# Wider DMA rows for q, k and the first values of a fused attention and feed-forward kernel

## The chip, the cores and the metric

One Trainium2 chip, one core. The metric is the device time of one execution in microseconds (us). Each kernel is executed several times, and each time is compared with runs of the kernel before on the same chip. Most kernels were also profiled once; span, timeline and waits come from that one execution.

## The reference

```python
def _attn_ref(q, k, v):                       # q, k, v: (8, 8, 576, 64) float32
    B, H, S, D = q.shape; chunk = 64; nc = S // chunk
    ...                                       # q_c, k_c, v_c: reshaped to (B, H, nc, chunk, D)
    scores = scale * np.matmul(q_c, k_c.transpose(0, 1, 2, 4, 3))
    ...                                       # softmax over the 64 keys of the chunk
    out = np.matmul(attn, v_c)

def _moe_ref(x, w_in, w_out):                 # x: (4608, 512), w_in: (512, 2048), w_out: (2048, 512)
    h = np.maximum(x @ w_in, 0.0)
    return (h * h @ w_out).astype(np.float32)
```

Every chunk of 64 tokens attends to itself alone. The outputs of the 8 heads are laid side by side as x, and x goes through the feed-forward network.

## The kernel before

The kernel takes the tokens in groups of 256. For each group it loads q, k and v, transposes q and k on TensorE, computes scores, their exponential (ScalarE), the value products (TensorE), the division (VectorE), and the transpose of x; then it runs the feed-forward matmuls for blocks of two groups. Groups 0 and 1 are done ahead of all feed-forward work ("the prologue"); the others are slipped between feed-forward matmuls. `keep_busy(n)` issues n matmuls of the identity, whose results nobody reads ("fillers").

For groups 0 to 3, q and k are each a tile of all 128 partitions, two tokens to a partition, so that each head gives a row of 512 B in DRAM:

```python
def qk_pieces(g):
    q_sb = in_pool.tile([128, 2, H, D], FP32, name="q_sb")
    k_sb = in_pool.tile([128, 2, H, D], FP32, name="k_sb")
    ...
            for dst, src in ((q_sb, q), (k_sb, k)):
                yield lambda ...: nc.sync.dma_start(
                    out=dst...[p:p + m // 2, :]...,
                    in_=src[b, :, s:s + m, :].rearrange("h (s i) d -> s h (i d)", i=2))
```

Values come in rows of 256 B, one token each, and the value products take 64 keys, that is 64 rows of the array, at a time:

```python
        for t in tiles:
            ...
            for hp in range(n_hp):
                for a in range(2):
                    for p in range(2):
                        c = p ^ a
                        vb = vob[t + p] if a else veb[:, t]
                        nc.tensor.matmul(
                            out=ps[64 * p:64 * p + 64, a, hp * (D + 1):(hp + 1) * (D + 1)],
                            lhsT=e[64 * c:64 * c + 64, a, hp, t, :],
                            rhs=vb[64 * c:64 * c + 64, hp, 1::2], start=True, stop=True)
            ...
            nc.vector.reciprocal(out=rec, in_=o[:, :, :, D])      # the sum, from a column of ones
            nc.vector.tensor_tensor(... op=ALU.mult)
```

The prologue, in TensorE's program order (TE: transposes of q and k; SC: scores; AV: value products of a tile of 128 tokens):

```python
    go(pieces([0, 1]))
    load_w_in(0, n_cast=2)
    TE(0); keep_busy(8); SC(0); keep_busy(6)
    TE(1); keep_busy(8); SC(1); keep_busy(10)
    AV(0, [0]); keep_busy(4); AV(0, [1]); keep_busy(8)
    transpose_x_early(0, 0); keep_busy(10); transpose_x_early(0, 1)
    AV(1, [0]); keep_busy(8); AV(1, [1])
    transpose_x_early(1, 0); keep_busy(14); transpose_x_early(1, 1); keep_busy(10)
```

The softmax here doesn't subtract the row's maximum and nothing guards it: scores larger than these inputs give would overflow.

Of the kernel before, what the change touches and what calls it, by code (L numbers as in the profile page):

```python
# [10 lines left out]
FP32 = mybir.dt.float32  # L11
# [6 lines left out]
def kernel(  # L18
# [19 lines left out]
    GT = 256  # L38
    n_grp = n_tokens // GT

    blocks = [[0, 1], [3, 2]] + [[g, g + 1] for g in range(4, n_grp, 2)]
    FIRST_DMA_T = 4
    FIRST_DMA_X = 6
    BT = GT * max(len(b) for b in blocks)
# [22 lines left out]
    NO = 2 * NV + 1  # L67
    v_even = [w_pool.tile([128, 2, n_hp, D + 1], FP32, name=f"ve_sb{i}") for i in range(NV)]
    v_odd = [w_pool.tile([128, n_hp, D + 1], FP32, name=f"vo_sb{i}") for i in range(NO)]
    for vt in v_even:  # L70
        nc.gpsimd.memset(vt[:, :, :, D:D + 1], 1.0)
    for vt in v_odd:
# [12 lines left out]
    def runs(g):  # L85

        for t in range(GT // 128):
            p = 0
            for b, s, m in segments(g * GT + t * 128, 128):
                yield t, p, m, b, s  # L90
                p += m

    def qk_pieces(g):
        q_sb = in_pool.tile([128, 2, H, D], FP32, name="q_sb")
        k_sb = in_pool.tile([128, 2, H, D], FP32, name="k_sb")
        qk[g] = (q_sb, k_sb)
        if g < FIRST_DMA_T:

            p = 0
            for b, s, m in segments(g * GT, GT):  # L100
                for dst, src in ((q_sb, q), (k_sb, k)):
                    yield lambda dst=dst, src=src, b=b, s=s, p=p, m=m: nc.sync.dma_start(  # L102
                        out=dst.rearrange("p t h d -> p (t h d)")[p:p + m // 2, :].rearrange(
                            "p (h e) -> p h e", h=H),
                        in_=src[b, :, s:s + m, :].rearrange("h (s i) d -> s h (i d)", i=2))
                p += m // 2
            return
        for t, p, m, b, s in runs(g):
            for dst, src in ((q_sb, q), (k_sb, k)):
                yield lambda dst=dst, src=src, b=b, s=s, t=t, p=p, m=m: nc.sync.dma_start(  # L110
                    out=dst[p:p + m, t, :, :],
                    in_=src[b, :, s:s + m, :].rearrange("h s d -> s h d"))

    def v_pieces(g):

        for t, p, m, b, s in runs(g):
            yield lambda t=t, p=p, m=m, b=b, s=s: nc.sync.dma_start(  # L117
                out=v_even[g % NV][p:p + m, t, :, 0:D],
                in_=v[b, 0::2, s:s + m, :].rearrange("h s d -> s h d"))
        for n in {0: [0, 1, 2], 2: [5], 3: [6, 7, 8]}.get(g, [2 * g + 1, 2 * g + 2]):  # L120
            lo, hi = max(0, 128 * n - 64), min(n_tokens, 128 * n + 64)
            p = lo - (128 * n - 64)
            for b, s, m in segments(lo, hi - lo):
                yield lambda n=n, p=p, m=m, b=b, s=s: nc.sync.dma_start(  # L124
                    out=v_odd[n % NO][p:p + m, :, 0:D],
                    in_=v[b, 1::2, s:s + m, :].rearrange("h s d -> s h d"))
                p += m
# [25 lines left out]
            place[g] = (j, i * GT)  # L153
    state = {}

    def transpose_paired(g, which, psb):

        src = qk[g][which].bitcast(BF16).rearrange(
            "p t h d -> p (t h d)").rearrange("p (h i d) -> p h i d", h=H, i=2)
        dst = psb.rearrange("c (h i q) -> c h i q", h=n_hp, i=2)  # L160
        for hp in range(n_hp):
            for i in range(2):
                for a in range(2):
                    nc.tensor.transpose(
                        out=dst[64 * a:64 * a + 64, hp, i, :],
                        in_=src[:, 2 * hp + a, i, 1::2],
                        identity=ident)

    def copy_paired(copy, qkT, psb):
        src = psb.rearrange("c (h i t p) -> c t h p i", h=n_hp, i=2, t=2)  # L170
        dst = qkT.rearrange("c t h (p i) -> c t h p i", i=2)
        for t in range(2):
            copy(out=dst[:, t], in_=src[:, t])

    def transpose_qk(g, q_pool, k_pool):
        qkT = att_pool.tile([128, 2, 2, n_hp, 128], BF16, name="qkT", bufs=4)
        state["qkT", g] = qkT
        for which, pool in enumerate((q_pool, k_pool)):
            copy = nc.scalar.copy if which else nc.vector.tensor_copy
            if pool is ps_ffn:  # L180
                bank = pool.tile([128, 512], FP32, name="ps_ffn")
            else:
                bank = pool.tile([128, 1024], FP32, name="ps_att")
            bank = bank.bitcast(BF16)[:, 0:1024]
            transpose_paired(g, which, bank)
            copy_paired(copy, qkT[:, which], bank)

    def transpose_x_early(g, t):
        j, c = place[g]
# [33 lines left out]
    def scores(g):  # L223
        qkT = state.pop(("qkT", g))
        ps = ps_att.tile([128, 1024], FP32, name="ps_att")
        for hp in range(n_hp):
            for t in range(2):
                for a in range(2):
                    for p in range(2):
                        c = p ^ a  # L230
                        cols = slice(p * 64, p * 64 + 64)
                        o0 = a * 512 + hp * 128 + t * 64
                        nc.tensor.matmul(  # L233
                            out=ps[64 * c:64 * c + 64, o0:o0 + 64],
                            lhsT=qkT[64 * a:64 * a + 64, 1, t, hp, cols],
                            rhs=qkT[64 * a:64 * a + 64, 0, t, hp, cols],
                            start=True, stop=True)
        e = att_pool.tile([128, 2, n_hp, 2, 64], BF16, name="e")
        state["e", g] = e
        nc.scalar.activation(  # L240
            out=e.rearrange("p a h t q -> p (a h t q)"), in_=ps, func=AF.Exp, scale=scale)

    def values(g, tiles=(0, 1)):
# [5 lines left out]
        x = state["x", g]  # L249
        for t in tiles:  # L250
            ps = ps_att.tile([128, 2, 512], FP32, name="ps_att")
            for hp in range(n_hp):
                for a in range(2):
                    for p in range(2):
# [5 lines that stand above are left out]
                            rhs=vb[64 * c:64 * c + 64, hp, 1::2],  # L260
                            start=True, stop=True)
# [30 lines left out]
    SC, AV, XT = scores, values, transpose_x  # L292

    def TA(g):
        transpose_qk(g, ps_att, ps_att)

    def TE(g):
        transpose_qk(g, ps_ffn, ps_ffn)

    def TM(g):  # L300
        transpose_qk(g, ps_att, ps_ffn)

    def XE(g):
        for t in range(2):
# [80 lines left out]

    go(pieces([0, 1]))
    load_w_in(0, n_cast=2)
    TE(0)
    keep_busy(8)
    SC(0)  # L390
# [112 lines left out]
```

## Time and profile before

| | before |
|---|---|
| time, median of 3 runs | 299.43 us (298.48 to 302.96) |
| the profiled execution | 296.57 us, span 294.8 us |
| first feed-forward matmul | 20.40 us |
| from there to the end | 274.4 us |

### The profile page before, as it was taken

How to read it: one execution, taken by the hardware profiler on the slowest of the kernel's cores; microseconds unless marked ns; L12 is line 12 of the kernel's file. 1: busy time of each engine (PE TensorE's matmuls, PEld its weight loads, DVE VectorE, ACT ScalarE, POOL GpSimd, SP SyncE). 2: the span in 40 equal slices, each digit the busy share in tenths (PEclk: the TensorE clock that was granted, in tenths of full speed). 3: DMA queues.
4: the chain of work that ended last, by engine and by line, in shares of the span. 5: the costliest groups of instructions: out<-in, count | busy, mean ns of one | idle time of the engine just before them, and what ended most of it. 6: DMA issues, size and time to landing. Idle time of an engine off the chain costs nothing.

```text
span 294.8 us, 6460 instructions
## 1 busy us (share of the span) xinstructions
PE 282.4 (96%) x2630; PEld 142.2 (48%) x2630; DVE 112.5 (38%) x246; ACT 130.9 (44%) x226; POOL 67.8 (23%) x103
## 2 busy tenths in 40 slices
PE   2999999899999999999999999999999999999994
PEld 1774445786454444444444444444444444444441
DVE  1157713594334520461047106720661046104300
ACT  1526514684327612771276127612761276126411
POOL 2027834050060052034104213311221100110010
PEclk9999999999999999999999999999999999999999
DMA  7999999999999999999999899799997401210011
GB/s 200 236 316 361 345 326 209 279 225 201 231 220 222 228 230 226 237 196 194 250 225 207 198 275 234 126 174 277 246 161 161 130 36 38 71 73 36 0 71 71
DMA packets 156140, 57.03 MB, mean 193 GB/s; under 512 B 139280, under 2 KB 151824, under 8 KB 156112
## 3 DMA queue, kind: packets, MB, share of 16 engines
q1 hardware_dynamic: 153168, 47.33, 77.5%
q0 software_dynamic: 2800, 9.18, 9.1%
q8 instruction: 20, 0.33, 0.5%
q10 hardware_dynamic: 144, 0.13, 0.1%
q14 instruction: 8, 0.07, 0.1%
HBM read 36.70 MB, written 9.44 MB: 157 GB/s over the span
## 4 chain that ended last, share of the span: by engine, by line
PE 74%; DMA 10%; SPq 8%; DVE 3%; issue 2%; ACT 1%; POOL 1%; ACTq 0%
PE ps_ffn L332 36%; PE ps_ffn L316 34%; DMA w_st<-in_moe_w_in_dram 5%; DMA k_sb<-in_k_dram 2%; SPq L124 2%; SPq L102 2%; DMA w_st<-in_moe_w_out_dram 2%; DVE gT L323 2%; PE ps_att L257 2%; SPq L117 2%; PE ps_att L233 1%; DMA qkT<-qkb 1%; ACT rl L322 1%; DVE x L265 1%; POOL w_in_bf L139 1%
## 5 line engine op out<-in xcount | busy, mean ns | idle before, releaser
L316 PE MATMUL ps_ffn<-xT,w_in_bf 128*128 128x512 bf16 (+1 forms) x640 | 128.9, 358 | 0.2 <-ACT rl L322 0.2
L323 DVE TENSOR_TENSOR gT<-rl 128x512 bf16<-128x512 bf16 (+1 forms) x160 | 75.3, 488 | 128.0 <-ACT rl L322 126.2
L332 PE MATMUL ps_ffn<-w_out_bf,gT 128*128 128x512 bf16 x512 | 112.9, 379 | 0.0
L322 ACT ACTIVATE rl<-ps_ffn 128x512 bf16<-128x512 f32 (+1 forms) x160 | 86.6, 557 | 37.7 <-PE ps_ffn L316 33.8
L316 PEld LDWEIGHTS <-w_in_bf 128*128 128x128 bf16 x640 | 61.0, 98 | 60.0 <-issue 0.5
L332 PEld LDWEIGHTS <-gT 128*128 128x128 bf16 x512 | 49.3, 98 | 58.0
L349 ACT COPY o_sb<-ps_ffn 128x512 f32<-128x512 f32 x31 | 18.2, 586 | 91.5 <-PE ps_ffn L332 91.5
L350 POOL DMA_DIRECT2D out_dram<-o_sb x31 | 16.7, 540 | 130.6 <-ACT o_sb L349 123.9
L212 POOL CAST qkb<-q_sb 128x1024 bf16<-128x1024 f32 x14 | 14.9, 1066 | 58.0 <-DMA q_sb<-in_q_dram 47.3
L265 DVE TENSOR_TENSOR x<-ps_att,rec 128x512 bf16<-128x512 f32 x36 | 24.9, 691 | 1.2
L240 ACT ACTIVATE e<-ps_att 128x1024 bf16<-128x1024 f32 x18 | 17.8, 1024 | 4.8 <-PE ps_att L233 4.8
L212 POOL CAST qkb<-k_sb 128x1024 bf16<-128x1024 f32 x14 | 15.2, 1082 | 2.4 <-DMA k_sb<-in_k_dram 2.1
L361 PE MATMUL ps_ffn<-w_out_bf,gT 128*128 128x512 bf16 x64 | 14.7, 379 | 0.0
L139 POOL CAST w_in_bf<-w_st 128x1024 bf16<-128x1024 f32 (+1 forms) x9 | 9.0, 1002 | 19.5 <-DMA w_st<-in_moe_w_in_dram 19.5
L264 DVE RECIPROCAL rec<-ps_att 128x8 f32<-128x8 f32 x36 | 7.1, 198 | 16.0 <-PE ps_att L257 16.0
L147 POOL CAST w_out_bf<-w_st 128x1024 bf16<-128x1024 f32 x8 | 9.0, 1122 | 6.0 <-DMA w_st<-in_moe_w_out_dram 5.8
L257 PEld LDWEIGHTS <-e 64*64 64x64 bf16 x576 | 6.4, 107 | 7.2 <-ACT rl L322 1.7
L361 PEld LDWEIGHTS <-gT 128*128 128x128 bf16 x64 | 6.0, 98 | 7.2 <-issue 0.3
L257 PE MATMUL ps_att<-ve_sb,e 64*64 64x65 bf16 x288 | 8.7, 196 | 0.1
L233 PEld LDWEIGHTS <-qkT 64*64 64x64 bf16 x576 | 6.0, 110 | 5.7 <-issue 4.2
L257 PE MATMUL ps_att<-vo_sb,e 64*64 64x65 bf16 x288 | 8.7, 196 | 0.0
L233 PE MATMUL ps_att<-qkT 64*64 64x64 bf16 x576 | 7.7, 197 | 1.0 <-DMA qkT<-qkb 0.6
(34 smaller groups left out, 55.0 us busy)
## 6 DMA issues: line engine op xcount, KB each, us to landing
out_dram<-o_sb POOLq DMA_DIRECT2D x35, 256.0 KB, 3.6
q_sb<-in_q_dram SPq DMA_DIRECT2D x25, 256.0 KB, 4.9
k_sb<-in_k_dram SPq DMA_DIRECT2D x25, 256.0 KB, 4.9
ve_sb<-in_v_dram SPq DMA_DIRECT2D x32, 128.0 KB, 4.0
vo_sb<-in_v_dram SPq DMA_DIRECT2D x32, 128.0 KB, 3.9
w_st<-in_moe_w_in_dram SPq DMA_DIRECT2D x8, 512.0 KB, 7.3
w_st<-in_moe_w_out_dram SPq DMA_DIRECT2D x8, 512.0 KB, 6.1
q_sb<-in_q_dram SPq DMA_DIRECT2D x3, 512.0 KB, 6.7
```

The costliest lines, as they stand in the source:

```text
L212: nc.gpsimd.tensor_copy(out=qkb[:, which], in_=qk[g][which].rearrange("p t h d -> p (t h d)"))
L233: nc.tensor.matmul(out=ps[64 * c:64 * c + 64, o0:o0 + 64], lhsT=qkT[64 * a:64 * a + 64, 1, t, hp, cols], rhs=qkT[64 * a:64 * a + 64, 0, t, ...
L240: nc.scalar.activation(out=e.rearrange("p a h t q -> p (a h t q)"), in_=ps, func=AF.Exp, scale=scale)
L257: nc.tensor.matmul(out=ps[64 * p:64 * p + 64, a, hp * (D + 1):(hp + 1) * (D + 1)], lhsT=e[64 * c:64 * c + 64, a, hp, t, :], rhs=vb[64 * c: ...
L265: nc.vector.tensor_tensor(out=x[:, t].rearrange("p h a d -> p a h d"), in0=o[:, :, :, 0:D], in1=rec.to_broadcast([128, 2, n_hp, D]), op=AL ...
L316: nc.tensor.matmul(out=h[:, 0:n], lhsT=w_in_bf[:, dt, ft * 128:(ft + 1) * 128], rhs=xT[:, c // 128:(c + n) // 128, dt, :], start=(dt == 0) ...
L322: nc.scalar.activation(out=rl[:, 0:n], in_=h[:, 0:n], func=AF.Relu)
L323: nc.vector.tensor_tensor(out=gT[:, ft, c:c + n], in0=rl[:, 0:n], in1=rl[:, 0:n], op=ALU.mult)
L332: nc.tensor.matmul(out=o_ps, lhsT=gT[:, ft, tt * 128:(tt + 1) * 128], rhs=w_out_bf[:, ft, :], start=(ft == 0), stop=(ft == n_ft - 1))
L349: nc.scalar.copy(out=o_sb, in_=o_ps)
L350: nc.gpsimd.dma_start(out=out[t0:t0 + 128, :], in_=o_sb)
L361: nc.tensor.matmul(out=o_ps[tt], lhsT=gT[:, ft, tt * 128:(tt + 1) * 128], rhs=w_out_bf[:, ft, :], start=(ft == 0), stop=(ft == n_ft - 1))
```

## The change

The intent is fewer and longer DMA rows, so that the first loads land sooner. For groups 0 to 3, q and k share a tile, q in partitions 0 to 63 and k in 64 to 127, with four tokens to a partition and rows of 1 KB. For groups 0 and 1, the values come in rows of 512 B of two tokens; the keys of a chunk then lie in 32 partitions as even and odd ones, so that scores and value products are done with 32-key tiles and accumulated, on top of a product of zeros that opens the accumulation, and the two halves of the sum are added by VectorE. Forty fillers are put ahead of the first transposes. The core of the diff:

```diff
     def qk_pieces(g):
-        q_sb = in_pool.tile([128, 2, H, D], FP32, name="q_sb")
-        k_sb = in_pool.tile([128, 2, H, D], FP32, name="k_sb")
+        qk_sb = in_pool.tile([128, 2, 2, H, D], FP32, name="qk_sb")
...
-                for dst, src in ((q_sb, q), (k_sb, k)):
...
-                        in_=src[b, :, s:s + m, :].rearrange("h (s i) d -> s h (i d)", i=2))
-                p += m // 2
+                for p0, src in ((p, q), (64 + p, k)):
+                    yield lambda dst=qk[g], src=src, b=b, s=s, p=p0, m=m: nc.sync.dma_start(
+                        out=dst[p:p + m // 4],
+                        in_=src[b, :, s:s + m, :].rearrange("h (s i) d -> s h (i d)", i=4))
+                p += m // 4
...
     def v_pieces(g):
+        if g < N_PAIRED:                      # N_PAIRED = 2
...
+                yield lambda b=b, s=s, p=p, m=m: nc.sync.dma_start(
+                    out=v_pair[g][p:p + m // 2, :, 1:2 * D + 1],
+                    in_=v[b, :, s:s + m, :].rearrange("h (s i) d -> s h (i d)", i=2))
...
     def scores(g):                            # 64 products of 32 keys for 32 of 64 keys
...
     def values(g, tiles=(0, 1)):
+            if g < N_PAIRED:
...
+                        nc.tensor.matmul(     # 2 x 2 of these
+                            out=ps[64 * p:64 * p + 64, a, 0:n_hp * E],
+                            lhsT=zeros[rows, 0:64], rhs=zeros[rows, 0:n_hp * E],
+                            start=True, stop=False)
...
+                                nc.tensor.matmul(   # 4 x 2 x 2 x 2 of these
+                                    out=ps[64 * p:64 * p + 64, a, hp * E + i:hp * E + i + D + 1],
+                                    lhsT=e[rows, a, hp, i, :],      # rows: 32 partitions
+                                    rhs=vp[rows, 2 * hp + a, ...],
+                                    start=False, stop=(i == 1 and hp == n_hp - 1))
...
+                nc.vector.tensor_copy(out=rec, in_=o[:, :, :, 0])
+                nc.vector.tensor_tensor(out=rec, in0=rec, in1=o[:, :, :, D + 1], op=ALU.add)
                 nc.vector.reciprocal(out=rec, in_=rec)
...
     load_w_in(0, n_cast=2)
+    keep_busy(40)
     TE(0)
```

## The prediction

> **What bounds the kernel now.** I read the page's shares first, then the chain of work that ended last, then TensorE's waits in the first 80 us, then the timeline up to 21 us. TensorE is busy 282.4 of 294.8 us. From 20.40 us on it runs the feed-forward matmuls almost without a hole, so two things remain to a change at the start: when that dense stretch begins, and the few waits after it. The waits of TensorE in 0 to 80 us, longest first (total us, times, longest):

> ```profile
> PE ps_ffn L164 <- DMA q_sb<-in_q_dram: 5.0, 1, 5.0
> PE ps_ffn L164 <- DMA k_sb<-in_k_dram: 1.8, 2, 1.1
> PE ps_att L233 <- DMA qkT<-qkb: 0.6, 1, 0.6
> ```

> 5.0 us is the first load; of the 1.8 us, 0.7 is the first k and 1.1 is the k of group 2, at 52.65 us. The prologue, in the timeline (start, us, engine, line):

> ```profile
> 5.02 1.06 PE L164 MATMUL ps_ffn<-ident,q_sb 128*64 128x128 bf16 x16 [5.02 <-DMA q_sb<-in_q_dram]
> 6.83 1.06 PE L164 MATMUL ps_ffn<-ident,k_sb 128*64 128x128 bf16 x16 [0.74 <-DMA k_sb<-in_k_dram]
> 7.82 1.03 PE L206 MATMUL ps_ffn<-ident 128*128 128x128 bf16 x8
> ...
> 10.33 1.06 PE L164 MATMUL ps_ffn<-ident,q_sb 128*64 128x128 bf16 x16
> ...
> 12.15 0.62 PE L206 MATMUL ps_ffn<-ident 128*128 128x128 bf16 x8
> ...
> 14.81 0.21 DVE L264 RECIPROCAL rec<-ps_att 128x8 f32<-128x8 f32 x1 [2.08 <-PE ps_att L257]
> ...
> 15.05 0.69 DVE L265 TENSOR_TENSOR x<-ps_att,rec 128x512 bf16<-128x512 f32 x1
> ...
> 20.40 13.97 PE L316 MATMUL ps_ffn<-xT,w_in_bf 128*128 128x512 bf16 x64
> ```

> See three things. Eight fillers take 1.03 us early and 0.62 us at 12.15: TensorE is slow until about 12 us. The transposes of group 1 start at 10.33 without waiting on a load, so up to there TensorE's own queue set the pace. And from the first value product (14.40 us) to the feed-forward there are 6.0 us, a chain product, VectorE, transpose, copy. Then the load rates, in stretches of 1 or 2 us (the last column is GB/s; q and k, then values, then w_in):

> ```profile
> 5.00:6.00 1.00, 0.98 (x16) 0.82 (x16) 0.00 (x0) 0.00 (x0) 0.00 (x0) 1.00 1.20 289
> 12.00:13.00 1.00, 0.87 (x18) 0.56 (x14) 0.73 (x2) 0.73 (x2) 0.00 (x0) 1.00 1.31 210
> 22.00:24.00 2.00, 2.00 (x11) 0.89 (x10) 1.34 (x3) 1.25 (x3) 1.61 (x2) 1.00 1.10 362
> 46.00:48.00 2.00, 2.00 (x41) 1.01 (x40) 0.00 (x0) 1.51 (x2) 0.00 (x0) 1.00 1.13 193
> ```

> 512 B rows run at 289 GB/s, 256 B rows at 210, the 1 KB rows of w_in at 362. The last is the stretch in which values and the q, k of group 2 queue.

> [...]per engine and packet they are 19.5, 28 and 45 ns for 256, 512 and 1024 B, a line with some 10 ns at zero. [...]The q and k of group 2 come as pieces of 32 and 96 partitions in the same 512 B rows. From issue plus time to landing they land at 48.36 (q, 32), 48.95 (k, 32), 50.74 (q, 96), 52.54 us (k, 96): 128 KB in 0.59 us is 222 GB/s, 384 KB in 1.80 us is 218, against 289 for whole tiles.[...]

> **The change, part by part.**

> 1. *q, k in 1 KB rows.* Half the packets, and by rows alone 1 MB would take 2.9 us at 362 GB/s instead of 3.6 us. But q goes to partitions 0 to 63 and k to 64 to 127, one transfer after the other. By the pieces above I take 220 to 235 GB/s: 4.5 us per group. Landings before, issue plus time to landing: q0 4.94, k0 6.74, q1 8.55, k1 10.47 us. After: the flow starts 1.8 us before 4.94, at 3.1; k0 lands at 7.6 and k1 at 12.1 us. Every first transpose now holds q and k rows, so it waits for k0, where before it began with q0 at 5.02.

> 2. *Fillers.* The identity is ready at 1.66 us. 40 fillers at 0.107 us end at 6.0. They replace idle time and cost nothing, but with k0 at 7.6 they stop short of it.

> 3. *Transposes and copies.* 32 transposes per group as before; one copy of 1024 columns instead of two of 512 on each engine. I count 1.2 us on VectorE (two took 1.29) and 1.05 on ScalarE (1.07): nothing.

> 4. *Scores of groups 0, 1.* 64 matmuls instead of 32. 64 took 0.64 us together in later blocks: +0.3 us each.

> 5. *Values in 512 B rows.* 1.0 MB instead of 1.06 MB, at 289 instead of 210 GB/s: 3.6 instead of 5.1 us. With k1 at 12.1, v0 lands at 13.9, v1 at 15.7, the first w_in at 17.2 instead of 18.1. So the later loads come 0.9 us sooner. This pays only if something waits for them.

> 6. *Value products.* Before, 16 matmuls per tile in four array tiles, stepping 0.04 us per four: 0.41 us to VectorE's start. After, 32 products in two array tiles, so 16 steps of 0.04 = 0.64, plus two rounds of the zero matmul with 264 columns (0.11 each) and 0.2 of latency: 1.07 us, +0.66. Two of the four tiles lie on the chain: +1.3 us. VectorE gets a copy and an add of 8 columns per tile; the reciprocal of that size takes 0.24 us start to start, so +0.48 us on each of four tiles in a row: +1.9 us. The chain from first value product to feed-forward grows from 6.0 to about 9.0 us.

> Now the path. Group 0 takes TensorE from 7.6 to about 12.0 (transposes 1.9 slow, copy 1.2, scores 0.7 and fillers). Group 1's transposes start at 12.1; copy, scores and ten fillers need 3.4 us more, so the first value product starts at 15.5, and the feed-forward at 24.5: **+4.1 us**.

> Later: group 3's q, k lose 1.1 us in the queue (1 MB at 230 instead of 289). Group 2's pieces now have 16 and 48 partitions[...]. TensorE gets there at 50.9 + 4.1 = 55.0 us. So the wait of 1.1 us shrinks to a few tenths: -0.6 us; the 0.6 us before the scores of group 4 may go too: -0.3. Sum: 4.1 - 0.9 = **+3.2 us**, 302.6 us.

> **Rivals.**

> *The rows win.* If q[...] and k[...] overlap, all runs at 360 GB/s: k0 at 6.1, k1 at 9.2. The 40 fillers end at 6.0, just then, as if tuned to it; that speaks for this rival. [...]the first value product starts at 12.6, and the feed-forward at 21.6: +1.2, less the whole 1.1 us wait: 299.5 us. Against it speak the 220 GB/s of the 32 and 96 partition pieces.

> *VectorE and the products cost less than I count.* If the small operations pipeline and the value products take 0.6 us, the chain is 7 us; with fast rows the feed-forward then starts at 19.6 and the time is some 297.5 us. The reciprocal's 0.24 us step is against it.

> *It is hidden anyway.* The start may be late without cost if w_in were the bound: each of its pieces arrives 0.5 to 1.8 us before use now, so it isn't, and a later start only gives it slack.

> **Range and chances.** I give the first account 0.55 (302.6), the fast rows 0.35 (299.5), the cheap chain 0.1 (297.5); their weighted mean is 301.1, and I say 301.3. The three runs before spread over 4.5 us. 297.5 to 305.0 holds most of all three. 2% is 6.0 us: slower than 305.4 needs the first account plus 3 us more (0.07); faster than 293.4 needs what none of them gives (0.02).

> **What would show it.** In the changed profile: the first transpose at 7.6 us rather than 6.1[...]; 4.5 or 2.9 us between the landing of the two k's; the value stretch near 289 GB/s; VectorE's four operations per tile, 1.3 us per tile; the first feed-forward matmul at 24.5, 21.6 or 19.6 us; and a wait at group 2's transposes of less than 1.1 us. The prediction is wrong above all if q and k to different halves do overlap, or if group 2's narrow pieces land later than I think and hold TensorE.

The prediction's sum is 4.1 - 0.9 = +3.2 us, so 302.6 us, but a term is cut from under it: what narrower pieces add to the last landing of group 2. Without that term this landing is at 52.5 - 0.9 + 1.1 = 52.7 us, ahead of TensorE's 55.0, and the wait would go by its whole 1.1 us instead of 0.6: a sum of +2.7 us. In part 1 the pieces give 218 and 222 GB/s; the upper end of "220 to 235", from which 4.5 us follows (1 MB at 233 GB/s), was the author's estimate and isn't shown.

## More of the kernel before

The page of the profile gives for each engine its busy time, its share of the span and its number of instructions, and for each DMA queue its packets, MB and share of 16 engines. Two of its lines:

```profile
PE 282.4 (96%) x2630; PEld 142.2 (48%) x2630; DVE 112.5 (38%) x246; ACT 130.9 (44%) x226; POOL 67.8 (23%) x103
...
q8 instruction: 20, 0.33, 0.5%
```

The first says that TensorE is full. The second looks idle: 20 packets, half a per cent of the DMA engines. By the queue's name these are instructions, and I take them for TensorE's program: 0.33 MB in 20 packets is 16 KB a packet, and 2630 matmuls with their 2630 weight loads are 5260 instructions, some 260 to a packet.

One stretch of the load rates, for later (columns: stretch, us, busy time and count of PE, PEld, DVE, ACT, POOL, granted clock of TensorE, DMA share, GB/s). In it loads of groups 2 and 3 are under way, by their packets mostly values in rows of 256 B:

```profile
42.00:44.00 2.00, 2.00 (x38) 1.28 (x37) 1.05 (x2) 0.60 (x2) 1.04 (x1) 1.00 1.19 300
```

## The result, and the profile after

The changed kernel took 315.15 us, median of 4 runs (313.98 to 319.52), against 300.1 us for the kernel before on the same chip: 1.050 times, with a 95% interval of 1.040 to 1.060. The prediction of 301.3 us, 297.5 to 305.0, was wrong. Here and below, a ratio is the mean time of one kernel's fast runs over the mean of the other's of the same rounds, so it is not quite the ratio of the medians.

The first profile of the changed kernel fell on its slowest execution (319.52 us, span 317.5). It was therefore run and profiled again without an edit: 314.36 us, span 312.3. That second profile is the one read here, and the first is named where it is used.

| | before | after |
|---|---|---|
| span of the profile | 294.8 us | 312.3 us |
| first feed-forward matmul | 20.40 us | 34.41 us (slow profile 35.16) |
| from there to the end | 274.4 us | 277.9 us (slow profile 282.3) |

So 14.0 of the 17.5 us were lost before the first feed-forward matmul. The prediction allowed 4.1 us there. TensorE's longest waits in the whole run (us in total, times, longest), fast profile of after:

```profile
PE ps_ffn L189 <- DMA qk_sb<-in_k_dram: 4.5, 2, 2.7
PE ps_ffn L377 <- DMA xT<-x: 3.4, 1, 3.4
PE ps_ffn L206 <- issue: 1.7, 1, 1.7
...
PE ps_att L245 <- issue: 1.5, 1, 1.5
```

The k loads are the first loads, as foreseen. The two lines "issue" are new: TensorE stood still and waited for nothing that the profile shows. The prologue in the timeline of the same profile (start, us, engine, line, operation, count, idle time before and what ended it):

```profile
8.89 1.08 PE L189 MATMUL ps_ffn<-ident,qk_sb 128*64 128x128 bf16 x32 [2.74 <-DMA qk_sb<-in_k_dram]
...
14.07 1.92 PE L189 MATMUL ps_ffn<-ident,qk_sb 128*64 128x128 bf16 x32 [1.72 <-DMA qk_sb<-in_k_dram]
...
16.88 0.39 PE L245 MATMUL ps_att<-qkT 64*32 64x64 bf16 x32
18.78 0.32 PE L245 MATMUL ps_att<-qkT 64*32 64x64 bf16 x32 [1.51 <-issue]
...
19.69 0.41 PE L285 MATMUL ps_att<-zeros 32*64 32x264 bf16 x4
...
20.68 0.17 DVE L303 COPY rec<-ps_att 128x8 f32<-128x8 f32 x1 [4.28 <-PE ps_att L294]
...
21.31 0.69 DVE L307 TENSOR_TENSOR x<-ps_att,rec 128x512 bf16<-128x512 f32 x1
...
25.53 0.37 PE L206 MATMUL ps_ffn<-ident,x 128*128 128x128 bf16 x2 [1.72 <-issue]
...
28.78 1.03 PE L217 MATMUL ps_ffn<-ident 128*128 128x128 bf16 x8
...
34.41 1.89 PE L377 MATMUL ps_ffn<-xT,w_in_bf 128*128 128x512 bf16 x8
```

Read it from the top. Group 0 starts at 8.89 us and group 1 at 14.07 us: both later than predicted, and both behind the load of k. In the middle of group 1's 64 scores TensorE stops for 1.51 us. VectorE then does what was predicted: from 20.68 to 22.00 are 1.32 us for its four operations. But between the second and the third of four x transposes TensorE stops again, for 1.72 us, and it stays slow: eight fillers take 1.03 us, as long as the first eight of the kernel before in its slow state. (The clock is on record from some time into the run, 12.1 us in the profile of before; ahead of that the views print 1.00, and only the length of the fillers tells.) The windows of this profile say the same, and show the loads:

```profile
14.00:15.00 1.00, 0.93 (x18) 0.96 (x20) 0.00 (x0) 0.00 (x0) 0.00 (x0) 0.50 1.20 289
...
28.00:30.00 2.00, 2.00 (x44) 1.68 (x40) 1.00 (x4) 0.00 (x0) 1.54 (x2) 0.50 1.08 369
...
42.00:44.00 2.00, 2.00 (x11) 0.94 (x10) 0.98 (x3) 1.31 (x3) 0.00 (x0) 1.00 1.14 144
```

The values run at the predicted 289 GB/s; q and k had run at 200 to 207 GB/s in the stretches from 6 to 12 us; the clock of 0.50 in that line follows the 2.74 us in which TensorE waited for the first k, and it was back at 1.00 by 17 us. At 28 to 30 us TensorE is busy for the whole 2 us, but its clock is granted at 0.50. At 42 to 44 us the loads of groups 2 and 3 run at 144 GB/s, where before 300 were reached. In the same profile the instruction queue has grown:

```profile
q8 instruction: 22, 0.36, 0.5%
```

### The profile page after: what moved, and what is told of

Same layout as the page of the kernel before. It is cut to its first block, busy times and chain, and to the rows that moved or that the text cites. A ratio compares the mean times of both kernels' runs of the same rounds, so it can differ in the third digit from the quotient of the medians.

```text
span 317.5 us, 6824 instructions
## 1 busy us (share of the span) xinstructions
PE 297.5 (94%) x2814; PEld 154.4 (49%) x2814; DVE 112.4 (35%) x250; ACT 130.6 (41%) x222; POOL 67.4 (21%) x108
## 4 chain that ended last, share of the span: by engine, by line
PE 80%; DMA 10%; SPq 5%; issue 2%; DVE 1%; POOL 1%; ACT 1%; POOLq 0%; ACTq 0%
PE ps_ffn L377 35%; PE ps_ffn L393 31%; PE ps_ffn L422 5%; DMA qk_sb<-in_k_dram 4%; PE ps_ffn L217 2%; SPq L230 2%; PE ps_att L318 2%; DMA xT<-x 2%; DMA qk_sb<-in_q_dram 2%; DMA vo_sb<-in_v_dram 1%; PE ps_att L258 1%; DMA qkT<-qkb 1%; PE ps_att L294 1%; SPq L134 1%; DVE gT L384 1%
## 5 line engine op out<-in xcount | busy, mean ns | idle before, releaser
L377 PE MATMUL ps_ffn<-xT,w_in_bf 128*128 128x512 bf16 (+1 forms) x640 | 132.3, 365 | 5.9 <-DMA xT<-x 5.7
L384 DVE TENSOR_TENSOR gT<-rl 128x512 bf16<-128x512 bf16 (+1 forms) x160 | 73.7, 475 | 137.4 <-ACT rl L383 135.3
L377 PEld LDWEIGHTS <-w_in_bf 128*128 128x128 bf16 x640 | 62.0, 99 | 68.1 <-issue 10.9
L410 ACT COPY o_sb<-ps_ffn 128x512 f32<-128x512 f32 x31 | 18.1, 585 | 91.9 <-PE ps_ffn L393 91.9
L411 POOL DMA_DIRECT2D out_dram<-o_sb x31 | 16.7, 539 | 133.4 <-ACT o_sb L410 133.4
L223 POOL CAST qkb<-qk_sb 128x1024 bf16<-128x1024 f32 x28 | 29.9, 1081 | 64.8 <-DMA qk_sb<-in_q_dram 57.3
L326 DVE TENSOR_TENSOR x<-ps_att,rec 128x512 bf16<-128x512 f32 x32 | 22.1, 692 | 1.1
L265 ACT ACTIVATE e<-ps_att 128x1024 bf16<-128x1024 f32 x18 | 17.7, 1023 | 7.9 <-PE ps_att L245 4.2
L217 PE MATMUL ps_ffn<-ident 128*128 128x128 bf16 x126 | 14.6, 299 | 1.7 <-POOL ident L61 1.7
L422 PE MATMUL ps_ffn<-w_out_bf,gT 128*128 128x512 bf16 x64 | 14.7, 380 | 0.0
L217 PEld LDWEIGHTS <-ident 128*128 128x128 bf16 x126 | 12.2, 140 | 2.3 <-POOL ident L61 1.7
L164 POOL CAST w_out_bf<-w_st 128x1024 bf16<-128x1024 f32 x8 | 8.3, 1040 | 13.6 <-DMA w_st<-in_moe_w_out_dram 13.6
L318 PE MATMUL ps_att<-vo_sb,e 64*64 64x65 bf16 x256 | 7.7, 196 | 0.4 <-DMA vo_sb<-in_v_dram 0.3
L197 ACT COPY qkT<-ps_ffn 128x1024 bf16<-128x1024 bf16 x3 | 3.0, 1012 | 11.5 <-PE ps_ffn L189 11.5
L318 PE MATMUL ps_att<-ve_sb,e 64*64 64x65 bf16 x256 | 7.7, 196 | 0.0
```

The source lines that it names most:

```text
L217: nc.tensor.matmul(out=ps[:, 0:128], lhsT=ident, rhs=ident, start=True, stop=True)
L223: nc.gpsimd.tensor_copy(out=qkb[:, which], in_=qk[g][which].rearrange("p t h d -> p (t h d)"))
L265: nc.scalar.activation(out=e.rearrange("p a h t q -> p (a h t q)"), in_=ps, func=AF.Exp, scale=scale)
L318: nc.tensor.matmul(out=ps[64 * p:64 * p + 64, a, hp * (D + 1):(hp + 1) * (D + 1)], lhsT=e[64 * c:64 * c + 64, a, hp, t, :], rhs=vb[64 * c: ...
L326: nc.vector.tensor_tensor(out=x[:, t].rearrange("p h a d -> p a h d"), in0=o[:, :, :, 0:D], in1=rec.to_broadcast([128, 2, n_hp, D]), op=AL ...
L377: nc.tensor.matmul(out=h[:, 0:n], lhsT=w_in_bf[:, dt, ft * 128:(ft + 1) * 128], rhs=xT[:, c // 128:(c + n) // 128, dt, :], start=(dt == 0) ...
```

## The experiments

Four theories were to be told apart.

- **Half tiles**: the halves cost rate, not the rows. q alone fills partitions 0 to 63 and k alone 64 to 127, and these loads ran at 200 to 207 GB/s, where whole tiles with 512 B rows had 289.
- **Instruction fetch**: TensorE stops (1.51 and 1.72 us in after_again) because the next 256 instructions of its program haven't arrived. The change adds 184 matmuls, so with their weight loads 368 instructions, ahead of the feed-forward, and this moves the borders between such blocks to places where a late block holds TensorE up.
- **Clock**: after idle time, or because the new value products keep few rows of the array at work, TensorE runs at half rate (a granted clock of 0.50) and its work in the prologue takes up to twice its time (one filler after the other every 0.107 us instead of 0.056).
- **Later loads**: q and k of groups 2 and 3 in half tiles arrive late for TensorE, in the middle of the feed-forward.

A simple rival to all of these is that the new instructions are just more work: more scores, more products, the zeros, the fillers.

Thirteen kernels were run: the first four on one chip, the next four, three and two on others. All are correct except the three that are said to be wrong. The columns of quoted lines are those explained above. The table has the whole, with the start of the feed-forward and the rest of the span from the profiled execution. The median is that of all runs, also those marked slow (two of four of qk_rows_only, one of four of qk_halves and of rows_g23):

| kernel | feed-forward starts | span | rest | median us | ratio to before (95%) |
|---|---|---|---|---|---|
| before | 20.40 | 294.8 | 274.4 | 299.43 | 1 |
| after_again | 34.41 | 312.3 | 277.9 | 313.84 | 1.044 (1.033 to 1.055) |
| qk_halves | 21.96 | 305.0 | 283.0 | 307.05 | 1.020 (1.009 to 1.031) |
| qk_rows_only | 22.63 | 306.9 | 284.3 | 309.51 | 1.021 (1.007 to 1.034) |
| values_only | 27.46 | 302.0 | 274.5 | 303.75 | 1.009 (1.002 to 1.017) |
| before_small | 22.20 | 297.4 | 275.2 | 299.66 | 1.004 (0.997 to 1.010) |
| after_wide | 31.20 | 312.3 | 281.1 | 313.11 | 1.045 (1.038 to 1.052) |
| values_64row | 22.92 | 296.4 | 273.5 | 298.38 | 0.997 (0.989 to 1.005) |
| pair_rows | 19.97 | 293.9 | 273.9 | 296.65 | 0.992 (0.986 to 0.997) |
| rows_g23 | 20.39 | 305.3 | 284.9 | 305.92 | 1.014 (1.006 to 1.022) |
| after_g23_full | 34.82 | 309.9 | 275.1 | 310.87 | 1.032 (1.025 to 1.040) |
| values_nozero | 26.33 | 298.9 | 272.6 | 301.47 | 1.002 (0.994 to 1.010) |
| after_no_fillers | 32.06 | 312.3 | 280.2 | 312.15 | 1.041 (1.034 to 1.048) |
| after_64row | 28.45 | 308.7 | 280.2 | 311.82 | 1.041 (1.030 to 1.052) |

### after_again: the changed kernel once more

No edit.

> The changed kernel once more, unedited, for a profile of a fast execution; the profiled one was slow (317.5 us). Theory: three things put the first feed-forward matmul at 35.2 us instead of 20.4: half-tile transfers (k of group 1 lands at 14.1 us), a stop of 2.9 us in the middle of the scores of group 1 that lies exactly 256 TensorE instructions before a second stop (an instruction fetch that comes late), and a TensorE clock of 0.50 from then on. If these are the kernel's own, a fast execution shows all three again at the same instructions, the feed-forward at 34 to 36 us and about 314 us in all; the 5.7 us wait for xT at 130 us should then be smaller or gone. Rival: the stop and the clock are chance of the one execution, and a fast one shows the feed-forward near 27 us.

It gave 314.36 and 313.32 us, and the profile read above. The two stops with no named wait and the half clock are there in both profiles of this kernel. What varies is their size: in the slow profile the first stop was longer, the second only 0.5 us.

```profile
19.35 0.42 PE L245 MATMUL ps_att<-qkT 64*32 64x64 bf16 x32 [2.91 <-issue]
```

The place is the same to the instruction: after 32 of group 1's 64 scores. Counting weight loads and matmuls in TensorE's program order, the first matmul after the stop is the 446th instruction (its weight load, the 445th, is recorded just before the stop), and the first after the other stop, amid the x transposes, is the 702nd: 256 apart. I call the two places the borders at 445 and 701; in the other kernels a stop falls up to two instructions later, again 256 apart wherever there are two. In the trace, an instruction packet starts at 16.2 us and TensorE goes on at 18.78 us; the next starts at 22.9 and TensorE goes on at 25.53. In the slow profile the pairs are 16.7 and 19.35, 23.4 and 26.09. So TensorE goes on some 2.6 us after the packet has started, four times of four.

### qk_halves: the rows of before, in halves

```diff
-                for dst, src in ((q_sb, q), (k_sb, k)):
+                n = m // 4
+                for dst, src, u in ((q_sb, q, 0), (k_sb, k, 1), (k_sb, k, 0), (q_sb, q, 1)):
...                                  # dst[p + u * n:p + u * n + n], 512 B rows as before
```

> The kernel before, its 512 B rows kept, but each q and k tile of groups 0 to 3 loaded as two transfers of 64 partitions, alternating between partitions 0 to 63 and 64 to 127. Theory[...]: the first 2 MB move at about 200 GB/s instead of 289, the transposes of group 1 start at about 14 us instead of 10.3, the feed-forward at about 24 instead of 20.4, and the time is 303 to 306 us. Rival, that the slow transfers of the changed kernel come from its 1 KB rows of four tokens (order of reads in memory) or from its fillers: the first 2 MB stay at about 289 GB/s and the time at 300 us.

Every row stays 512 B, but each transfer fills 64 partitions, by turns the lower and the upper ones.

```profile
6.00:8.00 2.00, 0.00 (x0) 0.00 (x0) 0.00 (x0) 0.00 (x0) 0.00 (x0) 1.00 1.21 229
...
12.71 0.64 PE L166 MATMUL ps_ffn<-ident,q_sb 128*64 128x128 bf16 x16 [0.47 <-DMA q_sb<-in_q_dram]
```

The rate is 229 GB/s instead of 289 for the same rows in whole tiles, and group 1's transposes start at 12.71 instead of 10.33 us. The half tile costs the rate, and that transfers to the two halves alternate doesn't win it back. This speaks for the half tiles and against "the rows win". The transfers are also half as large here, 256 KB; that size isn't the cause is seen in the changed kernel, whose transfers have 512 KB as before and run at 200. The expectation had the direction right and made the loss too large (200 GB/s, 14 and 24 us). The kernel is 2.0% slower although its feed-forward starts only 1.6 us late: the rest of the run is 8.6 us longer, with one wait of 6.9 us for q of group 3, at 50.80 us. That was the first sign of the later loads.

### qk_rows_only: only the q, k part of the change

```diff
-    N_PAIRED = 2
+    N_PAIRED = 0
...
-    keep_busy(40)
```

(To the changed kernel; the tables of value tiles as before.)

> The changed kernel's q, k part alone (1 KB rows in half tiles, mixed transposes, one copy per engine), with the values of the kernel before and without the 40 fillers. Theory: transposes of group 1 at about 14.1 us, the clock stays at 1.00, the instruction boundary falls on the value products of group 1 and costs nothing, the chain from first value product to feed-forward stays at 6 to 6.5 us: feed-forward at 24 to 24.5 us, 302 to 305 us in all. Rival, that the transfers explain most of the 15 us: feed-forward above 30 us and 310 us or more.

Group 1's transposes start at 13.46 us and the feed-forward at 22.63, only 2.2 us later than before. There is no stop between, and no fall of the clock. The loss lies later, and the expected time of 302 to 305 us was missed: the rest takes 9.9 us longer, with 8.8 us in three waits:

```profile
PE ps_att L187 <- DMA qk_sb<-in_k_dram: 5.8, 2, 2.9
...
PE ps_ffn L375 <- DMA xT<-x: 3.0, 1, 3.0
```

So the half tiles alone don't explain the 14 us of the changed kernel's prologue, and in this profile groups 2 and 3 lose more than groups 0 and 1.

### values_only: only the values part

The value tiles, the scores and the value products of the change on the kernel before (the diff of the change without its q, k part and without the forty fillers).

> The kernel before with the changed values, scores and value products of groups 0 and 1 alone (512 B rows, 32-key tiles); q, k as before, no fillers. Theory: q, k land as before (transposes of group 1 at 10.3 us); the 512th instruction falls into the fillers ahead of the first value product and its fetch[...] may stop TensorE there by 0 to 3 us; the products themselves cost 3 us on the chain at full clock (feed-forward at 23.5 to 25, 302 to 305 us), or, if 32-row tiles don't hold the clock, the clock falls to 0.50 and the feed-forward starts at 27 to 30 (307 to 310 us). Rival, that the values part is harmless and only the q, k part costs: feed-forward at or before 20.4 us and at most 300 us.

From the first value product (15.85 us) to VectorE (16.83) are 0.98 us where 1.07 was predicted, and VectorE's four operations take 1.33 us as predicted. Yet the feed-forward starts 7.1 us late:

```profile
15.70 0.22 PE L222 MATMUL ps_ffn<-ident 128*128 128x128 bf16 x1 [1.65 <-issue]
...
18.00:20.00 2.00, 2.00 (x27) 1.93 (x22) 1.38 (x5) 0.40 (x1) 1.32 (x2) 0.50 1.12 353
```

That is the 448th instruction, here a filler; the 704th, 256 later, follows a stop of 0.7 us and starts at 22.44 us. The granted clock falls to 0.50 twice, at 17.6 to 21.0 and 24.4 to 27.8 us, which in the kernel before doesn't happen once it has risen at 12.1 us. So the values part brings the stops and the slow clock, and of the late start it brings the larger part. The time shows less of it than expected of 7 us: 0.9%.

### before_small: only more instructions

```diff
     def keep_busy(n):
-        for _ in range(n):
-            nc.tensor.matmul(out=ps[:, 0:128], lhsT=ident, rhs=ident, ...)
+        for _ in range(2 * n):
+            nc.tensor.matmul(out=ps[:, 0:64], lhsT=ident, rhs=ident[:, 0:64], ...)
```

> The kernel before, with each 128-column filler matmul cut into two of 64 columns: the same TensorE time, 172 more TensorE instructions ahead of the feed-forward. Theory of the instruction fetch: TensorE's instructions come in blocks of 256[...]. In program order the blocks end at instructions 445 and 701. So TensorE should stop without a named wait 6 products into the second value tile (at about 15 us, for 1 to 2 us) and again in the last fillers, and the feed-forward starts at 23.5 to 25 us instead of 20.4. Rival: instructions are fetched well ahead, the stops of the changed kernel are a hidden semaphore wait; then no stop is seen and the feed-forward starts at 20.2 to 21 us. Second question, the clock: if idle gaps alone lower it, 0.50 shows after the first stop; if it takes the 32-row products, it stays at 1.00.

Each filler becomes two of half the columns: the same columns, 172 more instructions, and nothing else of the change.

```profile
18.50 0.83 PE L206 MATMUL ps_ffn<-ident 128*128 128x64 bf16 x23
21.06 0.31 PE L206 MATMUL ps_ffn<-ident 128*128 128x64 bf16 x5 [1.73 <-issue]
```

A stop of 1.73 us appears in the middle of 28 equal, independent fillers. Nothing that such a filler reads or writes can hold the 24th and not the 23rd. By the count it is the 704th, as in values_only; the packet had started at 18.8 us. This is the clearest sign that the stop comes from the program and not from the work. At the 445th there was no stop, though one was expected: its packet started at 11.1 us, and it was executed at 14.9, nearly four microseconds later. The stops came at a border that TensorE reached within some 2.6 us of the packet's start. The borders ahead of the feed-forward that went without a stop agree: there TensorE came 2.7 us after the packet's start (second border of values_64row) to 5.0 us (first border of before). The clock stays at 1.00, the feed-forward starts at 22.20 us, sooner than expected, and the time doesn't change measurably: 1.8 us at the start cost nothing here.

### after_wide: the changed kernel with fewer instructions

```diff
     def keep_busy(n):
-        for _ in range(n):
-            nc.tensor.matmul(out=ps[:, 0:128], lhsT=ident, rhs=ident, ...)
+        for _ in range((n + 2) // 4):
+            nc.tensor.matmul(out=ps, lhsT=ident, rhs=ident4 as 512 columns, ...)
```

> The changed kernel with its fillers as 512-column matmuls, a quarter as many: about the same TensorE time, 184 instructions fewer before the feed-forward, so only two block boundaries (445 and 701, now 11 products into the first value tile and in the last value tile) lie ahead of it instead of two with a third close by, and the stop inside the scores of group 1 goes. Theory: no stop in the scores, a stop of at most 1.5 us in the first value tile; feed-forward at 26 to 31 us instead of 34.4 to 35.2, time 305 to 311 us. Rival, that transfers and the slow clock alone set the start: still 33 us or later and 313 us.

With 184 instructions fewer the border falls into the first tile of the value products, and so does the stop:

```profile
PE ps_att L298 <- issue: 2.7, 1, 2.7
```

There is none left in the scores. The feed-forward starts 3.2 us sooner than in after_again, but the time is the same, 313.11 us, and not the expected 305 to 311: 3.5 us of wait for x of a later group, and 2.6 us for values, stand in the rest of the run. In this profile the earlier start was lost again in waits for later loads.

### values_64row: the values part with the products of before

```diff
-                for a in range(2): ...        # the products of zeros
-                for i in range(2): ...        # 32 products of 32 rows
+                            nc.tensor.matmul(  # 16 products of 64 rows, as in the kernel before
+                                out=ps[64 * p:64 * p + 64, a, hp * E:(hp + 1) * E],
+                                lhsT=e[64 * c:64 * c + 64, a, hp, t, :],
+                                rhs=vp[64 * c:64 * c + 64, 2 * hp + a, 1:2 * (D + 1):2],
+                                start=True, stop=True)
```

It is values_only otherwise, with the four VectorE operations. The result is wrong, as the keys and values no longer match.

> Values alone, but with value products of 64 rows in four array tiles over the same tiles, no zero matmuls, VectorE's four operations kept (a wrong result on purpose). Up to the scores of group 1 its TensorE program is that of the values-alone kernel, so the stop at instruction 445 of about 1.6 us at 14 us stays. Theory: [...]the clock stays at 1.00 here, and the chain from first value product to feed-forward is 8 us (6.0 plus 4 times 0.48), not 11.6. Rival: the idle stop lowers the clock; then it falls to 0.50 at about 17.8 us here as well.

The theory was that the 32-row products and the products of zeros hold the clock down. The stop at the first border is still there, 1.09 us, but the clock, once risen, never falls:

```profile
18.00:20.00 2.00, 1.71 (x49) 1.16 (x46) 1.41 (x6) 0.31 (x1) 1.49 (x2) 1.00 1.11 350
```

The feed-forward starts at 22.92 instead of 27.46 us. So this stop of 1.09 us alone didn't lower the clock, and 64-row products with the same loads and the same VectorE work go without it. Of the late start of 7.1 us, 4.5 go with the products: their shape, their number (16 for 32) and the zeros changed together, and the stop is 0.6 us shorter. (Two runs.)

### pair_rows: 1 KB rows over all partitions

```diff
+    pair_sb = [w_pool.tile([128, H, 4 * D], FP32, name=f"pair_sb{i}") for i in range(2)]
...
+            for dst, src in zip(pair_sb, (q, k)):     # q of groups 0 and 1, then k of both
+                yield lambda dst=dst, src=src: nc.sync.dma_start(
+                    out=dst, in_=src[0, :, 0:2 * GT, :].rearrange("h (s i) d -> s h (i d)", i=4))
...
-    TE(0)
+    transpose_pair(0, 0); transpose_pair(0, 1); keep_busy(14)
+    transpose_pair(1, 0); transpose_pair(1, 1)
     keep_busy(8)
     SC(0)
     keep_busy(6)
-    TE(1)
-    keep_busy(8)
     SC(1)
```

> A version that keeps what was good in the idea: q and k of groups 0 and 1 as one tile each in 1 KB rows over all 128 partitions (two transfers of 1 MB), values as before, no half tiles. Theory[...]: 1 MB lands in 2.9 to 3.1 us, q at about 6.1 and k at about 9.1 us, scores of both groups from 12 us, feed-forward at 19 to 20.5 us, the first w_in a microsecond earlier; 297 to 300 us, that is 0 to 1.3% faster than before. Rival, that rows of four tokens are slow in themselves: k lands after 10.5 us, feed-forward at 21.5 us or later, 301 us or more.

This gives the long rows without the halves. Transfers are twice as large (1 MB), the transposes of both groups come first, and there are six more fillers; values, scores and the loads of groups 2 and 3 are untouched.

```profile
6.00:8.00 2.00, 1.81 (x32) 1.68 (x32) 0.71 (x2) 0.00 (x0) 0.00 (x0) 1.00 1.05 352
...
9.64 1.92 PE L207 MATMUL ps_ffn<-ident,pair_sb 128*64 128x128 bf16 x32
```

The rate is 352 GB/s, all 2 MB of q and k are in by 9.3 us (before 10.47, after 13.97), and the time is 296.65 us over six runs, 0.8% below before, with an interval that lies below 1. It is the fastest correct kernel. The feed-forward starts only 0.4 us sooner than before, so most of these 0.8% have no place in the profile yet, and that they come from the rows is not shown. The rate is: long rows are faster, and the half tiles took this away.

### rows_g23: half tiles for groups 2 and 3 alone

```diff
     def qk_pieces(g):
+        if not g in (2, 3):
+            yield from qk_pieces_full(g)              # as before
+            return
...                                                   # 1 KB rows in half tiles, as in the change
```

> The kernel before with 1 KB half-tile rows, mixed transposes and single copies for groups 2 and 3 alone; groups 0 and 1 and all values as before. Theory: the prologue is untouched (feed-forward at 20.4 us), but the loads of groups 3 and 2 run at 150 to 220 GB/s between 34 and 56 us instead of 330 falling to 200, TensorE waits 4 to 8 us in all for q, k of group 3 and 2 and later for xT, and the time is 303 to 307 us, most of what the q, k part alone cost (8 us). Rival, that the later start of the prologue is what the q, k part costs: 298 to 300 us here.

The prologue is that of before: the feed-forward starts at 20.39 us. The time grows by 1.4%, and the profiled run waits:

```profile
PE ps_att L245 <- DMA qk_sb<-in_k_dram: 6.1, 2, 5.7
```

```profile
42.00:44.00 2.00, 0.58 (x3) 0.08 (x1) 0.00 (x0) 0.00 (x0) 0.00 (x0) 1.00 1.14 159
```

The k of group 3 lands at 48.2 us, and TensorE is ready for it at 42.6. The rate was 300 GB/s at this time before, and is 159 now; but such a stretch depends on what is queued in it (values_only and pair_rows, with whole tiles here, have 178 and 175). The surer measure is the transfer itself, 512 KB of k of group 3 from issue to landing (the last number, us), in the kernel before and here:

```profile
k_sb<-in_k_dram SPq DMA_DIRECT2D x1, 512.0 KB, 8.4
...
qk_sb<-in_k_dram SPq DMA_DIRECT2D x1, 512.0 KB, 14.4
```

In after_again it took 16.1 us, in after_g23_full, with whole tiles again, 8.5. The prediction had 0.9 us of gain here.

### after_g23_full: the changed kernel without that part

```diff
     def qk_pieces(g):
+        if not g < 2:
+            yield from qk_pieces_full(g)              # as before
+            return
```

> The changed kernel with groups 2 and 3 back on 512 B rows over 128 partitions and their transposes and copies of before; its prologue is unedited. Feed-forward should start at 33.5 to 35.5 us again. Theory A, the late prologue is what costs (14 us later start): 311 to 314 us. Theory B, the changed kernel is bound by loads after its late prologue (starting 3.2 us earlier with wide fillers gained nothing): 305 to 309 us, with the waits for xT and vo_sb after 100 us gone.

The prologue is as late as in after (34.82 us), but the rest takes 275.1 us, nearly that of before, and no wait for x or values is left. (In after_again it is one wait for x, 3.4 us at 132.3 us, that makes up nearly all of the 3.5 us by which its rest is longer than before.) The load rate is back:

```profile
42.00:44.00 2.00, 2.00 (x11) 0.94 (x10) 1.29 (x4) 1.47 (x3) 0.07 (x1) 1.00 1.11 332
```

The time falls between the two theories, and the ratio is 1.032. So some 10 us of the changed kernel's loss (3.2% of 300.9) belong to the prologue, and about 4 us to groups 2 and 3: 1.4% in rows_g23, and 1.2 to 1.7 points between the 1.044 and 1.050 of the changed kernel and this 1.032. The intervals of the last two touch, so the 4 us rest more on rows_g23 than on that difference.

### values_nozero: are the products of zeros the trouble?

```diff
-                for a in range(2): ...                # the four products of zeros
...
-                                    start=False, stop=(i == 1 and hp == n_hp - 1))
+                                    start=True, stop=True)
```

It is values_only otherwise. The result is wrong: nothing is accumulated.

> Values alone without the zero matmuls, each 32-row product starting its own sum (a wrong result on purpose). It tells which of the two lowers TensorE's clock. If the 32-row products do: 0.50 again in two stretches between 17 and 28 us, feed-forward at 26 to 28 us. If the zero operands do: clock at 1.00 throughout, no filler slower than 0.056 us after 13 us, feed-forward at 23 to 24.5 us. Stops at instruction 445 (1 to 2 us) and 701 in both cases.

The feed-forward starts at 26.33 us, 1.1 us sooner than in values_only, and the clock still falls to 0.50 once, from 18.2 to 21.6 us. The products of zeros account for part of the work, and the clock falls without them; the second fall of values_only is gone. (Two runs.)

### after_no_fillers: the forty fillers taken out

```diff
     load_w_in(0, n_cast=2)
-    keep_busy(40)
     TE(0)
```

> The changed kernel without the 40 fillers ahead of the first transposes, 80 TensorE instructions fewer. I had counted them as free. Theory of the instruction blocks: the stop at instruction 445 moves from the middle of the scores of group 1 to the last fillers ahead of the first value product and shrinks to 1 to 1.5 us, the one at 701 moves into the first value tile of group 1, and the third block boundary (957, with the fillers just ahead of the feed-forward) falls into the feed-forward: its start at 28 to 31 us instead of 34.4 to 35.2, the time 306 to 311 us. If the fillers were needed for the clock, it is at 0.50 for longer and the start stays at or after 34 us. Rival, that they are free: start at 34 to 35.5 us, 313 to 315 us.

The fillers were to cost nothing. Without them the feed-forward starts 2.4 us sooner:

```profile
20.50 0.27 PE L217 MATMUL ps_ffn<-ident 128*128 128x128 bf16 x2 [2.29 <-issue]
```

The first border has moved out of the scores into the last fillers before the first value product, and there is no stop at the second. The clock is back at 1.00 by 27.7 us. The start, 32.06 us, lies between what the theory and the rival said. The time, 312.15 us, isn't told apart from that of the changed kernel.

### after_64row: the changed kernel with 64-row products

The edit of values_64row on the changed kernel. Its output is wrong, which doesn't matter for the time.

> The changed kernel with value products of 64 rows in four array tiles and no zero matmuls, VectorE's four operations kept (a wrong result on purpose). Up to the scores of group 1 its TensorE program is the changed kernel's, so the stop there (1.5 to 2.9 us) should stay. If the 32-row products hold the clock down, it is at 1.00 from 17 us on or recovers within 4 us after the stop, the chain from first value product to feed-forward is 8 to 9 us instead of 14.3 and the feed-forward starts at 27 to 29 us. If the stop alone does it, the clock stays at 0.50 for 10 us or more and the feed-forward starts at 31 us or later.

The stop in the scores is there as in the slow profile of after, 2.91 us long, and the clock falls at 18.9 us, ahead of the first value product, so here the stop brings the fall. But it recovers at 22.3 us, where the changed kernel stays at 0.50 until 34 us or later in both profiles:

```profile
24.15 0.62 PE L217 MATMUL ps_ffn<-ident 128*128 128x128 bf16 x8
...
28.45 1.89 PE L367 MATMUL ps_ffn<-xT,w_in_bf 128*128 128x512 bf16 x8
```

Eight fillers take 0.62 us here and 1.03 us in after_again at the same point of the program. From the first value product (20.47 us) to the feed-forward are 8.0 us, against 14.7. The start is 6.0 us sooner, and the time hardly: 311.82 us (two runs), as TensorE then waits 2.7 us for k and 3.7 us for the scores' input. Waits for later loads take the place of the late start once more.

## Why the prediction was wrong

Taken by its own steps:

- **"I take 220 to 235 GB/s: 4.5 us per group"**. The direction was right, and the rival "the rows win" was not: qk_halves shows that halves lose rate at unchanged rows, and pair_rows that rows win once they span all partitions. The size was low: 4.5 us for 1 MB is the fast end of the range, 233 GB/s. 512 KB took 2.5 to 2.7 us, that is 197 to 210 GB/s, so k0 came at 8.7 us instead of 7.6, and k1 at 14.0 us instead of 12.1: 1.9 us. One reading behind it was wrong, too. The piece of 96 partitions lies in partitions 32 to 127, that is in both halves; at the 222 GB/s of the piece that does lie in one half, its larger part, 256 KB, would take an estimated 1.2 us and not the 1.80 measured, so it didn't speak for the halves.
- **"the first value product starts at 15.5"**. It started at 19.69 us. 1.9 of these 4.2 us are the load, and 1.5 the stop at the first border. The rest is in the sum: from the first transposes of group 1 to the first value product the prediction counts 3.4 us, where the kernel before had taken 4.07 (10.33 to 14.40), and the changed one takes 4.1 without the stop. No rival held instruction fetch, and the page's line of instruction packets was not read. The count of the added instructions was written down (part 4 and part 6 of the prediction), but only as work, never as positions in the program.
- **"The chain from first value product to feed-forward grows from 6.0 to about 9.0 us"**. It took 14.7 us. Its terms were right at full clock: in values_only 0.98 us for the products where 1.07 was said, 1.33 us on VectorE. What failed is the clock. With 64-row products the same chain took 8.0 us, a stop of 0.9 us included. The fall itself came with the first stop, in both kernels; with the 32-row products the clock then stayed at half rate through the whole chain, fillers included, and with 64-row ones it didn't. (In after_wide and after_no_fillers, with 32-row products too, it was back after 6.8 us; what decides is looked at below.) A further 1.7 us is the stop at the second border. In the profile TensorE is busy without a break from 28 to 34 us, and the fillers that had been free time became the queue that the feed-forward stood behind.
- **"They replace idle time and cost nothing"**. Not so at the start of the feed-forward, which comes 2.4 us sooner without them; the borders moved, and the slow clock lasted 6.8 us instead of 13.7. In the time this can't be told from nothing.
- **"So the later loads come 0.9 us sooner" and "the wait of 1.1 us shrinks"**. The reverse happened: rows_g23 alone costs 1.4%. The estimate treated the pieces of groups 2 and 3 as a queue at 230 GB/s; in fact the mean from 36 to 62 us was 178 GB/s, where the kernel before had 268, and the k of group 3 took 16.1 us from issue to landing instead of 8.4. The prediction named late narrow pieces as what could make it wrong, but as part of no sum.
- **Values at 289 GB/s, 1.3 us of VectorE per tile, transposes and copies for nothing, w_in not the bound**: as predicted. The first feed-forward matmuls run without a wait for w_in in all profiles.
- **Small slips without effect.** 6.0 + 1.3 + 1.9 is 9.2 and not 9.0 us, 1 MB at 230 instead of 289 GB/s is 0.9 and not 1.1 us, and the weighted mean is 301.0.
- **The range.** All three accounts moved the same terms by a few us, so their spread of 297.5 to 302.6 was that of one model. What could double a whole stretch, the clock, was cited and left at "the fillers agree".

**What is shown and what is inferred.** Shown: the stops' places, 256 instructions apart, their move when only the count of fillers changes, and the packet that starts 2.3 to 2.8 us ahead of where TensorE goes on. Not shown: when a block is asked for, and why it comes late; no run was made with the same borders and idle queues. Shown: with 32-row products the clock falls or stays low where it doesn't with 64-row ones, in two pairs of kernels. That the rows at work are what counts was inferred from them, and the pairs change the number of products and the stops as well.

**What stays open.** Why the loads at 36 to 62 us, with a mean of 178 GB/s, run even below the rate of a plain half tile (197 to 210 GB/s). Why the 14 us of late start cost only about 10 us in the timed runs: some of it is hidden, since before_small, values_64row and values_nozero (1.8, 2.5 and 5.9 us late) lost nothing measurable, but where was not found; the one profile of before, at 296.57 us, is also faster than its median, and may lack waits that its other executions have. And why the wait for x of a later group appears in some profiles and not in others.

## What to carry to other kernels

A transfer had to span all 128 partitions before longer rows paid: rows of 1 KB ran at some 200 GB/s in halves (after_again) and at 352 in full (pair_rows). In a short, dependent prologue, count where added instructions put the borders of 256 in TensorE's program (stops of 0.5 to 2.9 us here), and ask whether narrower matmul tiles let its clock fall (to 0.50 here), since then also the terms that were sized right take longer (eight fillers 1.03 us instead of 0.62). Undo one part at a time: here some 4 of 14 us of the loss came from groups 2 and 3, which a look at the prologue alone would have hidden.
